# Loading x ahead of its tables, in pieces of 112 and 14 rows, and reordering the first weights: FNet mixing with a sigmoid GLU on one core

## The chip, the cores and the metric

The kernel runs on one core of a Trainium2 chip. The core has five engines that run side by side, each in the order of its own instruction list: TensorE (PE, matmuls; weight loads are listed as PEld), VectorE (DVE), ScalarE (ACT), GpSimd (POOL) and SyncE (SP), which here issues nearly all DMA transfers. They wait for each other through semaphores. The metric is device microseconds of one execution. The time before is 1924.73 us, the median of three runs (1924.28 to 1924.87).

## The reference

The input x has 8 sequences of 3008 positions with 256 features. It goes through a Fourier transform along the positions and one along the features, of which the real part is kept; then every position goes through a feed-forward layer with 1536 hidden units.

```python
X = np.fft.fft(x, axis=1)            # x: (8, 3008, 256)
X = np.fft.fft(X, axis=2)
x = X.real.reshape(8 * 3008, 256)
gate = 1.0 / (1.0 + np.exp(-(x @ w_gate)))     # w_gate, w_val: (256, 1536)
val = x @ w_val
out = (gate * val) @ w_out                     # w_out: (1536, 256)
```

## The kernel before

The order of every engine's work is written out by hand: the program order of the Python code is the order on each engine. Between engines, semaphores hold an instruction until what it reads has been written. Transfers on SyncE's queue are issued in program order too, and a transfer that has to wait holds back all behind it.

**Sequence transform.** Sine and cosine tables (`stab`, 126 rows on partitions, 6 slots `q`, two tables `t`) are multiplied with folded x. Symmetry is used: x is folded (`fold_ops`, L440) by adding and subtracting mirrored positions and features, so that each table has 126 x 6 rows. For the first sequence this goes in three thirds, two slots `q` each (`N3` = 3). For each third j VectorE does `third` (L498, L499, L460) and `feats` (L505 to L508); ScalarE makes signed copies, `turned` (L510) and a one-column form of it (L516). TensorE then adds the third's share to the sums: `e0_sums` (the `pe` matmuls, first eight straight ones for each third, then eight that read the turned copies), and three groups of `half` (the `ev` and `od` matmuls). The straight sums of a third read table `t` 0 or 1; the turned sums of odd `q` read the other one. A fourth group follows once all thirds are there. VectorE then adds `ev` and `od` into `pk` and `qk` (`places`, L584, L588).

**Weights.** `weight_load(j)` (L257) loads a block of 256 x 256 values of w_gate, w_val (j 0 to 11) or w_out (12 to 17), 0.5 MB each, from the eight-byte numbers in which the weights are given. `weight_parts(j)` makes two passes on ScalarE (L309, L311), `weight_join(j)` three on VectorE (L322, L323, L325) and one addition on GpSimd (L327) to turn them into four-byte numbers. `merge` (called `piece` at the start) multiplies the block with the feature-transform table `dt`, four matmuls into `ps`, and `merged(j)` copies the result to G on ScalarE (L358). `ge_load(j)` (L371) sends parts of a row of G to a column form `ge`.

**The steady loop.** For each of the steps i, TensorE makes `pf` from `pk` (`front_a`) and from `qk` (`front_b`); `seed` (L729) and `part` (L740) run on ScalarE, `gate_a` holds a sigmoid (L754) and VectorE's z (L755), `gate_b` VectorE's L767, a second sigmoid (L768) and VectorE's L771; `back` does the output matmuls. What is done besides (a weight's parts, join and use) is put into lists by step number: `pre` and `use` run after the gates of the step, `mid` (the join) inside `gate_b` or, at step 1, behind it. The list of pairs at L1053 gives each weight's step.

**The start, in SyncE's order** (L948 to L956): weights 0 to 3; then for each third its part of x (`load_third`, 1 MB, 128 partitions) and its two tables (`load_table`, 126 partitions, two slots of 377 values: 371 KB each); then weights 4 and 5. Eight `ge` transfers come next and wait for G, then weights 6 to 12. `dt` (256 KB) is issued by ScalarE (L947). TensorE starts with matmuls on a constant tile (`warm`). ScalarE does parts 0, 1, 2, then the copy to G of weight 0, then parts 3, and the copies 1 and 2. The parts of weight 4 come between the signed copies of the second and the last third.

Of the kernel before, what the change touches and what calls it, by code (L numbers as in the profile page):

```python
# [54 lines left out]
NP = 126  # L55
# [27 lines left out]
def kernel(  # L83
# [10 lines left out]
    nc = tc.nc  # L94
    B, _, _, _, D = xf.shape
    F = moe_w_gate.shape[1]
    P = 128
# [3 lines left out]
    NE = (M // 2) // 2 + 1  # L101
# [9 lines left out]
    N3 = NQ // 2  # L111
# [33 lines left out]
    def load_x(b):  # L145
        X[b] = xp.tile([P, 4, NQ, D], F32, name="x4", tag="x4")
        if b:
            for h in range(0, 4, 2):
                nc.sync.dma_start(out=X[b][:, h : h + 2], in_=XR[b][:, h : h + 2])

    def load_third(j):

        q = slice(2 * j, 2 * j + 2)
        rows = xf.rearrange("b p h q d -> (b p) h q d")
        nc.sync.dma_start(out=X[0][:, :, q], in_=rows[0:P, :, q])
# [26 lines left out]
    dt = const.tile([P, 2, D], F32, name="dt")  # L182
    HE, HO = M // 8 + 1, M // 8
# [4 lines left out]
    ST = [st[:, 0:n].rearrange("p (t q k) -> p t q k", t=2, q=NQ)]  # L188
# [13 lines left out]
    wkeep = dram.tile([P, 4, D], F32, name="wkeep")  # L202

    def load_table(t, j):
        q = slice(2 * j, 2 * j + 2)
        nc.sync.dma_start(out=ST[0][0:NP, t, q, 0 : HE + HO], in_=stab[:, t, q, HO : NE + HO])

    def table_again():

# [47 lines left out]
    def weight_load(j):  # L257


        w, c = jobs[j]  # L260
        src = (moe_w_gate, moe_w_val, moe_w_out)[w]
        src = src[2 * c * P : 2 * (c + 1) * P, :] if w == 2 else src[:, c * WC : (c + 1) * WC]
        src = src.rearrange("(c p) f -> p c f", p=P)

        def some(n, pool, tag):

            if tag not in shared:
                shared[tag] = pool.tile([P, n * WC], F32, name=f"w{tag}", tag=tag)
            return shared[tag]

        def home(j):

            if j in (0, 1, 2, 10, 11):
                t = hp.tile([P, 6 * WC], F32, name="raw", tag="h")
                return t[:, 0 : 4 * WC], t[:, 4 * WC :]
            if j in (3, 4):
                ws = some(5, pqp, "qk")[:, (j - 3) * 2 * WC : (j - 2) * 2 * WC]
                return sp.tile([P, 4 * WC], F32, name="raw", tag="sf"), ws
            if j < 8:
                t = wf[:, j - 4].rearrange("p m n -> p (m n)")  # L280
                return t[:, 0 : 4 * WC], t[:, 4 * WC : 6 * WC]
            if j < 10:
                shared[j] = cp.tile([P, 10 * WC], F32, name="wc", tag="c")
                return shared[j][:, 0 : 4 * WC], shared[j][:, 4 * WC : 6 * WC]
            return (shared[8][:, 6 * WC :] if j == 12 else shared["qk"][:, 0 : 4 * WC],
                    shared[9][:, (6 + 2 * (j - 12)) * WC : (8 + 2 * (j - 12)) * WC])

        if j < KEEP:
            raw, ws = home(j)
        else:  # L290
            both = some(24, xp, "x4").rearrange("p (i n) -> p i n", n=2 * WC)
            i = 3 * (j - KEEP)
            raw, ws = both[:, i : i + 2].rearrange("p a n -> p (a n)"), both[:, i + 2]
        raw = raw.bitcast(I32).rearrange("p (c f w) -> p c f w", c=2, w=2)
        ws = ws.rearrange("p (c f) -> p c f", c=2)
        WS[j] = ws
        if src.dtype == F32:
            nc.sync.dma_start(out=ws, in_=src)
        else:
            RAW[j] = raw  # L300
            nc.sync.dma_start(out=raw.rearrange("p c f w -> p c (f w)"), in_=src.bitcast(I32))

    def weight_parts(j, which=(0, 1)):

        if j in RAW:
            raw, ws = RAW[j], WS[j]
            lo, hi = raw[:, :, :, 0], raw[:, :, :, 1]
            if 0 in which:
                nc.scalar.activation(ws, hi.bitcast(F32), AF.Abs)  # L309
            if 1 in which:  # L310
                nc.scalar.activation(lo, lo.bitcast(U32), AF.Copy, scale=2.0 ** -29)  # L311

    def weight_join(j, other=None):
        if j not in RAW:
            return
        raw, ws = RAW.pop(j), WS[j]
        lo, hi = raw[:, :, :, 0], raw[:, :, :, 1]
        wi = ws.bitcast(I32)
        mid_ = bank("join", other).rearrange("p (c f) -> p c f", c=2)
        mi = mid_.bitcast(I32)  # L320
        ts = nc.vector.tensor_scalar
        ts(out=mid_, in0=ws, scalar1=2.0 ** -15, scalar2=HUGE, op0=ALU.max, op1=ALU.min)  # L322
        ts(out=mi, in0=mi, scalar1=3, scalar2=0x3FFFFFF8, op0=ALU.logical_shift_left,  # L323
           op1=ALU.bitwise_and)
        nc.vector.scalar_tensor_tensor(out=wi, in0=hi, scalar=-(2 ** 30), in1=mi,  # L325
                                       op0=ALU.bitwise_and, op1=ALU.bitwise_or)
        nc.gpsimd.tensor_tensor(wi, wi, lo, op=ALU.add)  # L327
# [25 lines left out]
    def merged(j):  # L353

        g, c = jobs[j]
        ps = MERGED.pop((g, c))
        cs = slice(c * WC, (c + 1) * WC)
        nc.scalar.copy(G[:, :, g, cs], ps.rearrange("p (h n) -> p h n", h=2))  # L358
# [12 lines left out]
    def ge_load(j):  # L371
        for g, f in ge_at((j,)):
            nc.sync.dma_start(out=ge[:, g, f : f + 1], in_=G2[0:1, g, f * P : (f + 1) * P])
# [233 lines left out]
    def e0_sums(j):  # L607

        if not j:
            E0["ps"] = bank("pe", NB - 1)  # L610
        for q in (2 * j, 2 * j + 1):
            for blk in range(2):
                row = (2 * blk + q % 2) * TB
                mm(E0["ps"][row : row + 1, columns(blk)[0]], W[0, blk][2][:, q], table_of(0, q, blk), not j, j == N3 - 1)
        for q in (2 * j, 2 * j + 1):
            for blk in range(2):
                row = (2 * blk + q % 2) * TB
                mm(E0["ps"][row : row + 1, columns(blk)[1]], XV[:, blk, q, HD : HD + 1],
                   table_of(0, q, blk, True), False, j == N3 - 1)
# [324 lines left out]
    nc.gpsimd.memset(nil, 0.0)  # L944
    nc.scalar.activation(table, nil[:, 0, 0:1], AF.Sigmoid)
    nc.gpsimd.dma_start(out=zero, in_=nil)
    nc.scalar.dma_start(out=dt, in_=dtab.rearrange("(c p) d -> p c d", p=P))  # L947
    load_x(0)  # L948
    for j in range(4):
        weight_load(j)  # L950
    for j in range(N3):
        load_third(j)
        for t in range(2):
            load_table(t, j)
    for j in (4, 5):
        weight_load(j)  # L956

    def warm(n):
# [5 lines left out]
    def piece(j, other=None):  # L964
        merge(WS.pop(j), *jobs[j], other)
# [4 lines left out]
    for j in range(4):  # L970
        weight_parts(j)
        weight_join(j, j % 3)
        piece(j, (None, None, None, 3)[j])
        if j > 1:
            merged(j - 2)
    merged(2)
    for j in range(3):
        ge_load(j)
    seq_start(0)
# [3 lines left out]
    for j in range(N3):  # L983
        folds[2 * j]()
        e0_sums(j)
        if not j:
            merged(3)
            ge_load(3)
            for i in (6, 7, 8, 9, 10, 11, 12):
                weight_load(i)  # L990
        folds[2 * j + 1]()
        if j == 1:
            weight_parts(4)
        for sums, _, _ in halves:
            sums(2 * j, 2 * j + 1)
# [53 lines left out]
    def using(j):  # L1049
        weight_use(j, j % 2)  # L1050
        if jobs[j][0] < 2:
            merged(j)
    for j, i in ((11, 1), (12, 3), (13, 5), (14, 6), (15, 8), (16, 10), (17, 12)):  # L1053
        if j > 10:
            pre.setdefault(i - 1, []).append(lambda j=j: weight_parts(j))
        mid.setdefault(i, []).append(lambda j=j: weight_join(j, 2))
        if jobs[j][0] == 2:
            use.setdefault(i + 2, []).append(lambda j=j: using(j))
# [138 lines left out]
```

## Time and profile before

| | |
|---|---|
| median of 3 runs | 1924.73 us (1924.28 to 1924.87) |
| the profiled execution's own time | 1925.47 us |
| its span, from the first to the last instruction | 1923.70 us |
| TensorE busy | 1912.1 us, 99% of the span |
| weight loads / VectorE / ScalarE / GpSimd busy | 93% / 73% / 70% / 81% |
| TensorE's first matmul on a weight | 9.33 us |
| TensorE's first `pe` sums | 19.04 us |
| turned `pe` sums of the last third | 31.12 us |
| last wait of TensorE in the start-up | ends at 60.20 us |

The page gives, for one execution, each engine's busy time, the chain of work that ended last, groups of instructions and the transfers. The same trace can be asked for a stretch of time: an instruction's line then holds its start and duration in us, engine, line of the code, operation, what is written and read, the shape, the count, and in square brackets how long the engine had been idle before it and who ended that. A line of the waits holds who waited for whom: us in total, times, the longest. A line of the stages holds a stretch, its length, the busy time of PE, PEld, DVE, ACT and POOL with the number of instructions, the granted TensorE clock, the mean busy share of the 16 DMA engines, and GB/s.

### The profile page before, as it was taken

Reading aid. Unit: us, or ns where it says so; the run is one execution under the profiler, and the core shown is the slowest. Engines: PE = TensorE matmul, PEld = TensorE weight load, DVE = VectorE, ACT = ScalarE, POOL = GpSimd, SP = SyncE. Lnnn points to the kernel's source line nnn. Section 1 sums busy time; section 2 is a strip of 40 time slices with the busy share of each in tenths; the row PEclk is TensorE's granted clock in tenths of the full one; section 3 lists DMA queues with packets and bytes.
Section 4 is the critical chain, followed back from the end, with each engine's and each line's share of the span. In section 5 each row is a group of like instructions: output and inputs, shape, how many; then the busy total and the mean of one; then the engine's idle time right before and its main releaser. Section 6 shows DMA issues by size and latency. Waiting matters only on the chain.

```text
span 1923.7 us, 34664 instructions
## 1 busy us (share of the span) xinstructions
PE 1912.1 (99%) x11340; PEld 1793.4 (93%) x11340; DVE 1410.9 (73%) x3220; ACT 1346.3 (70%) x3158; POOL 1554.7 (81%) x2807
## 2 busy tenths in 40 slices
PE   8999999999999999999999999999999999999999
PEld 7899999999999999999999999999999999999998
DVE  7757876787767776777777777777777777766776
ACT  5877767767777677776777767777677766777775
POOL 2589989978898688986888878988788886777775
PEclk9999999999999999999999999999999999999999
DMA  9251421111020201202111020111200100000001
GB/s 305 84 91 37 106 80 57 51 62 33 20 77 26 80 18 36 68 15 80 25 48 49 20 81 21 47 51 24 80 14 15 26 16 15 15 22 20 26 17 30
DMA packets 169215, 95.62 MB, mean 50 GB/s; under 512 B 129658, under 2 KB 159940, under 8 KB 167244
## 3 DMA queue, kind: packets, MB, share of 16 engines
q1 hardware_dynamic: 168482, 92.90, 17.0%
q8 instruction: 91, 1.49, 0.3%
q14 instruction: 88, 0.72, 0.1%
q10 hardware_dynamic: 522, 0.50, 0.1%
q0 software_dynamic: 32, 0.00, 0.0%
HBM read 68.13 MB, written 47.24 MB: 60 GB/s over the span
## 4 chain that ended last, share of the span: by engine, by line
PE 96%; ACT 1%; POOL 0%; DVE 0%; issue 0%; ACTq 0%; POOLq 0%
PE pf L135 50%; PE po L135 41%; PE ev L135 2%; PE rows L135 1%; PE od L135 1%; PE row L135 0%; POOL sf L777 0%; ACT pf L729 0%; ACT G L358 0%; ACT ae L740 0%; PE pe L135 0%; ACT wf L311 0%; ACT wc L311 0%; PE ps L135 0%; POOL st L231 0%
## 5 line engine op out<-in xcount | busy, mean ns | idle before, releaser
L777 POOL TENSOR_TENSOR sf<-h 128x168 f32<-128x168 f32 (+1 forms) x935 | 516.7, 571 | 229.8 <-DVE h L771 229.2
L777 POOL TENSOR_TENSOR sf<-h,sf 128x168 f32<-128x168 f32 (+1 forms) x1122 | 614.0, 568 | 49.4 <-DVE h L771 47.9
L135 PE MATMUL pf<-qk,G 128*128 128x252 f32 (+1 forms) x2304 | 582.0, 375 | 1.3 <-ACT ae L740 1.3
L135 PE MATMUL pf<-pk,G 128*128 128x252 f32 (+1 forms) x2304 | 582.5, 376 | 0.0
L729 ACT ACTIVATE pf<-ek,ge 128x252 f32<-128x252 f32 (+1 forms) x1152 | 542.6, 471 | 19.3 <-DVE h L771 0.3
L771 DVE TENSOR_TENSOR h<-pf,z 128x252 f32<-128x252 f32 (+1 forms) x576 | 241.6, 419 | 415.2 <-ACT pf L768 413.6
L135 PE MATMUL po<-sf,wf 128*128 128x168 f32 (+1 forms) x2992 | 516.9, 306 | 0.3 <-POOL sf L777 0.2
L740 ACT ACTIVATE ae<-pf 128x504 f32<-128x504 f32 (+1 forms) x576 | 339.2, 589 | 249.2 <-PE pf L135 248.0
L135 PEld LDWEIGHTS pf<-pk,G 128*128 128x128 f32 x2304 | 437.0, 190 | 51.7 <-issue 2.0
L135 PEld LDWEIGHTS po<-sf,wf 128*128 128x128 f32 x2992 | 460.6, 190 | 9.2 <-POOL sf L777 1.0
L135 PE MATMUL po<-h,wf 128*128 128x168 f32 (+1 forms) x2618 | 463.3, 305 | 0.0
L135 PEld LDWEIGHTS pf<-qk,G 128*128 128x128 f32 x2304 | 410.8, 190 | 27.9 <-ACT ae L740 2.1
L755 DVE TENSOR_TENSOR z<-ae,pf 128x504 f32<-128x504 f32 (+1 forms) x576 | 386.0, 670 | 63.1 <-ACT h L754 58.3
L135 PEld LDWEIGHTS po<-h,wf 128*128 128x128 f32 x2618 | 416.6, 190 | 16.2
L895 DVE TENSOR_TENSOR c<-c 128x168 f32<-128x168 f32 (+1 forms) x929 | 423.5, 464 | 3.4
L754 ACT ACTIVATE h<-pf 128x252 f32<-128x252 f32 (+1 forms) x576 | 218.5, 379 | 208.5 <-PE pf L135 199.8
L767 DVE TENSOR_TENSOR h<-h,pf 128x252 f32<-128x252 f32 (+1 forms) x576 | 233.5, 405 | 0.0
L768 ACT ACTIVATE pf<-z 128x252 f32<-128x252 f32 (+1 forms) x576 | 211.4, 367 | 23.4 <-DVE h L767 20.1
L777 POOL TENSOR_TENSOR sf<-sf 128x168 f32<-128x168 f32 (+1 forms) x187 | 104.2, 557 | 14.7
L777 POOL TENSOR_TENSOR sf<-sf,h 128x168 f32<-128x168 f32 (+1 forms) x187 | 110.3, 590 | 0.0
L808 ACT COPY c<-po 128x504 f32<-128x504 f32 (+1 forms) x141 | 80.0, 568 | 0.0
L904 DVE STREAM_TRANSPOSE os<-c 128x256 f32<-128x256 f32 x184 | 79.9, 435 | 0.0
(168 smaller groups left out, 921.9 us busy)
## 6 DMA issues: line engine op xcount, KB each, us to landing
x<-xr SPq DMA_DIRECT2D x14, 1536.0 KB
out_dram<-os SPq DMA_DIRECT2D x368, 56.0 KB
xr<-in_xf_dram SPq DMA_DIRECT2D x14, 768.0 KB
xr<-in_xf_dram SPq DMA_DIRECT2D x35, 256.0 KB
ek<-ed SPq DMA_DIRECT2D x39, 126.0 KB
out_dram<-os SPq DMA_DIRECT2D x284, 7.0 KB
x<-in_xf_dram SPq DMA_DIRECT2D x3, 1024.0 KB
st<-in_stab_dram SPq DMA_DIRECT2D x4, 564.8 KB
```

The costliest lines, as they stand in the source:

```text
L135: nc.tensor.matmul(o, l, r, start=start, stop=stop, skip_group_check=True)
L729: nc.scalar.activation(PF[i][:, g], EK[i // NFT], AF.Copy, scale=ge[:, g, f : f + 1])
L740: nc.scalar.activation(AP[i], PF[i], AF.Copy, scale=2.0)
L754: nc.scalar.activation(H[p][:, fh, 0:n], PF[i][:, 0], AF.Sigmoid)
L755: nc.vector.tensor_tensor(z[:, :, ::-1], AP.pop(i), PF[i], op=ALU.subtract)
L767: nc.vector.tensor_tensor(h[:, fh, 0:n], h[:, fh, 0:n], pf[:, 1], op=ALU.mult)
L768: nc.scalar.activation(pf[:, 0], z[:, 0], AF.Sigmoid)
L771: nc.vector.tensor_tensor(h[:, fh, n:], pf[:, 0], z[:, 1], op=ALU.mult)
L777: nc.gpsimd.tensor_tensor(block(p, dst), block(p, a), block(p, b), op=(ALU.subtract, ALU.add)[op])
L808: (nc.vector.tensor_copy if t == 1 or t == 3 and not last else nc.scalar.copy)(C[0][:, 3 * t * R : 3 * (t + 1) * R], PO[t][:, 0 : 3 * R])
L895: engine.tensor_tensor(t[:, dst * R : (dst + 1) * R], *v, op=(ALU.subtract, ALU.add)[op])
L904: nc.vector.transpose(os_[0][:, s, 0:nb, h, :], t[:, c0 : c0 + nb * TB])
```

## The change

All three thirds of x are issued ahead of all tables. The table transfers are cut to rows 0 to 111, and the remaining rows 112 to 125 of a table, for all six slots, go in one transfer of their own (14 rows of 6 x 377 values) ahead of that table's first piece. Weight 4 is issued between the tables of the second and the last third, and weights 6 and 7 move up behind 5, ahead of the eight `ge` transfers. `dt` moves from ScalarE's queue to SyncE's, behind the second weight. On ScalarE the first three copies to G come after the parts of weight 3, and weight 11 moves one step later: its parts from step 0 to step 1, its join from step 1 to inside the gate of step 2. TensorE's and GpSimd's orders stay as they were; on VectorE only weight 11's join moves, behind the next z (L755) and L767.

```diff
     def load_table(t, j):
-        q = slice(2 * j, 2 * j + 2)
-        nc.sync.dma_start(out=ST[0][0:NP, t, q, 0 : HE + HO], in_=stab[:, t, q, HO : NE + HO])
+        q, rows = slice(2 * j, 2 * j + 2), slice(0, NP - NP % 16)
+        if not j:
+            last = slice(NP - NP % 16, NP)
+            nc.sync.dma_start(out=ST[0][last, t, :, 0 : HE + HO], in_=stab[last, t, :, HO : NE + HO])
+        nc.sync.dma_start(out=ST[0][rows, t, q, 0 : HE + HO], in_=stab[rows, t, q, HO : NE + HO])
...
-    nc.scalar.dma_start(out=dt, in_=dtab.rearrange("(c p) d -> p c d", p=P))
     load_x(0)
     for j in range(4):
         weight_load(j)
+        if j == 1:
+            nc.sync.dma_start(out=dt, in_=dtab.rearrange("(c p) d -> p c d", p=P))
     for j in range(N3):
         load_third(j)
+    for j in range(N3):
+        if j == N3 - 1:
+            weight_load(4)
         for t in range(2):
             load_table(t, j)
-    for j in (4, 5):
+    for j in (5, 6, 7):
         weight_load(j)
...
         piece(j, (None, None, None, 3)[j])
-        if j > 1:
-            merged(j - 2)
-    merged(2)
+    for j in range(3):
+        merged(j)
...
-            for i in (6, 7, 8, 9, 10, 11, 12):
+            for i in (8, 9, 10, 11, 12):
                 weight_load(i)
...
-    for j, i in ((11, 1), (12, 3), (13, 5), (14, 6), (15, 8), (16, 10), (17, 12)):
+    for j, i in ((11, 2), (12, 3), (13, 5), (14, 6), (15, 8), (16, 10), (17, 12)):
```

## The prediction

> **What bounds the kernel now.** I read the page's busy shares and its chain first, then TensorE's waits up to 70 us and from there on, then the timeline, engine by engine, of the first 60 us, then the DMA rate by stage.
>
> ```profile
> PE 1912.1 (99%) x11340; PEld 1793.4 (93%) x11340; DVE 1410.9 (73%) x3220; ACT 1346.3 (70%) x3158; POOL 1554.7 (81%) x2807
> PE 96%; ACT 1%; POOL 0%; DVE 0%; issue 0%; ACTq 0%; POOLq 0%
> ```
>
> TensorE works for 1912.1 us of 1923.7 and holds 96% of the chain. Its matmuls stay as many, and in the same order. So the change can only alter TensorE's idle time, 11.6 us in all. The next fence is TensorE's waits before 70 us (the first four lines) and after 70 us (the last one): us in total, times, longest.
>
> ```profile
> PE ps L135 <- POOL wqk L327: 1.7, 1, 1.7
> PE pe L135 <- ACT st L516: 1.4, 1, 1.4
> PE pf L135 <- ACT ae L740: 1.3, 1, 1.3
> PE ps L135 <- POOL raw L327: 0.9, 1, 0.9
> ...
> PE po L135 <- POOL sf L777: 0.2, 1, 0.2
> ```
>
> Everything that can be won stands in the first 61 us, and it is some 5 us, 0.28% of the time. The three waits that the change reaches are of 1.7, 1.4 and 1.3 us. From 60.20 on the chain is TensorE alone, so the forecast is a shift of that point. Now the two waits in the middle, from the timeline:
>
> ```profile
> 25.11 0.17 DVE L498 TENSOR_TENSOR x<-x 126x4 f32<-126x4 f32 x1 [1.23 <-DMA x<-in_xf_dram]
> 29.68 0.66 ACT L309 ACTIVATE wqk<-raw 128x512 f32<-128x512 f32 x1 [3.06 <-DMA raw<-in_moe_w_gate_dram]
> 30.78 0.29 ACT L516 ACTIVATE st<-x,sgn 126x4 f32<-126x4 f32 x1
> 31.12 0.50 PE L135 MATMUL pe<-st 126*1 126x188 f32 x8 [1.36 <-ACT st L516]
> ```
>
> VectorE waits for x's last third until 25.11. ScalarE then waits for weight 4 until 29.68, and `turned`'s first copy for the last third (L516), in order behind it, keeps TensorE until 31.12. The third wait:
>
> ```profile
> 50.83 0.68 ACT L309 ACTIVATE raw<-raw 128x512 f32<-128x512 f32 x1
> 51.97 0.37 ACT L754 ACTIVATE h<-pf 128x252 f32<-128x252 f32 x1
> 54.32 0.68 DVE L322 TENSOR_SCALAR join<-raw 128x512 f32<-128x512 f32 x1
> 56.38 0.67 DVE L755 TENSOR_TENSOR z<-ae,pf 128x504 f32<-128x504 f32 x1
> 57.41 0.38 ACT L768 ACTIVATE pf<-z 128x252 f32<-128x252 f32 x1 [1.80 <-DVE h L767]
> 60.20 1.12 PE L135 MATMUL pf<-qk,G 128*128 128x252 f32 x4 [1.32 <-ACT ae L740]
> ```
>
> Weight 11's halves (L309) stand ahead of gate 0 on ScalarE, and its join (54.32 to 56.38) ahead of gate 1 on VectorE. The DMA rate by stage (the last two columns are share and GB/s):
>
> ```profile
> 9.50:12.00 2.50, 2.45 (x11) 1.84 (x12) 2.39 (x4) 0.64 (x2) 1.28 (x1) 1.00 1.06 400
> 12.00:15.50 3.50, 3.36 (x15) 2.30 (x13) 2.88 (x7) 1.71 (x4) 1.96 (x2) 1.00 1.09 241
> 18.50:22.00 3.50, 3.48 (x31) 2.36 (x30) 3.40 (x6) 2.28 (x5) 0.00 (x0) 1.00 1.06 279
> ```
>
> x moves at 400 GB/s, the tables (12 to 15.5, 18.5 to 22) at 241 to 279, though the queues are full in all three stretches.
>
> **The change part by part.** Times are those of the profiled execution: 1925.47 us with 1.77 us around its span of 1923.70, 0.74 above the median of 1924.73. The shift is added to the median.
>
> *Tables behind x.* TensorE's sums of the first third need its tables as well as x. Before, both were there when TensorE came free, at 19.04. Now three thirds of x go first. By the DMA rates summed over half microseconds the first four weights and `dt` (2.36 MB) are through at 8.7. Three thirds (3.15 MB) at 400 GB/s take 7.9 us more: 16.6. Before, x's last third stopped moving at about 24.1 (the rate falls to 233 GB/s there) and was seen at 25.1, so I add 1.0 for the slowest part: x is in SBUF at 17.6. Then two pairs, 14 rows (127 KB) and 112 rows (338 KB), must land before the turned sums can start, since odd q use the other table.
>
> A 112-row transfer: at 400 GB/s 0.85 us; it can't cost more than a whole 126-row one. Of those, two and a weight fill 25.11 to 29.68. With 1.3 us for the weight (0.52 MB at 400) a table took 1.65. I take 1.3, its bytes at the 260 GB/s between the two table stretches. A 14-row transfer: 0.3 at 400 GB/s, or 1.65, a whole table's, if its few rows are no faster. No row is near it; I take 1.1, in the upper half, because these tables already ran well below the full rate.
>
> The second pair lands at 17.6 + 2 x (1.1 + 1.3) = 22.4; ends 17.6 + 2 x (0.3 + 0.85) = 19.9 and 17.6 + 4 x 1.65 = 24.2. Before, the turned sums started at 19.36. So TensorE starts them 3.0 us later, and idles from about 18 on.
>
> The Trainium skill speaks against the 14-row pieces: SBUF — State Buffer, "Door 1: the DMA port swizzle", puts partitions 112 to 125 on 4 of 16 write ports, at about 27 GB/s each. By that a piece would take an estimated 1.3 us (four rows of 9 KB on one port) and the pair would land at 22.8, the shift below 0.4 larger. The trace of before writes no such narrow range, so no run here shows it.
>
> *What the thirds then gain.* Before, the turned sums go from 19.36 (first third) to 31.12 (last), 11.8 us. With the tables of later thirds 1.3 us apart behind the first, x's folds done by about 27 (three folds of 4.2 to 5.1 us from 13.6) and weight 4 landed at about 26.4, ahead of ScalarE's need at 28.3, no wait is left but TensorE itself. 24.15 to 29.26 is one third, 5.1; 19.36 to 24.15 the first, 4.8; 0.3 for the straight sums; less 0.3 of small waits for VectorE: 9.9. The last third's turned sums then start at 22.4 + 9.9 = 32.3, against 31.12: **+1.2 us**. The 1.23 us of VectorE, the 3.06 us of ScalarE and TensorE's 1.36 are gone, paid for by the wait for tables. What follows to 50.04 hangs on these sums (VectorE's copies L644, at 31.74 before, then joins and places) and shifts whole.
>
> *Weight 11 one step later.* ScalarE: gate 0's sigmoid (L754) no longer waits for two halves (50.83 to 51.97) but for TensorE's `pf` (50.04 + 1.12): about 0.8 earlier. VectorE's z for it is held by weight 10's join (to 51.86): 0.5 earlier. Weight 11's halves (1.14) now come before gate 1's sigmoid, 55.0 for 54.35; but z of gate 1 no longer waits for the join: 55.4 for 56.38, L768 56.4 for 57.41, and L740, which TensorE awaits, 58.5 for 59.56. That is **-1.0 us**; bounds: 0, if the gate chain is held elsewhere, and -1.3, the whole wait. Behind the moved join waits gate 1's last product (L771), 58.5 for 57.83, read only by sums that run later. Weight 11's add on POOL ends near 60.0; TensorE asks near 60.8.
>
> *Parts that cost or bring nothing.* `dt` leaves ScalarE's queue (0.49 us of issue while ScalarE was idle till 4.99) for SyncE's: the first weights come up to 0.65 us sooner (0.26 MB at 400). Weight 3's halves no longer sit behind the first copy to G: they ran at 11.84, and could at about 9.5. Both let the join of weight 3 and the fold start about 1.1 us sooner and TensorE's fourth piece start at 16 instead of 17.11. Their cover is the wait for tables; with tables at 19.9 they would count. SyncE issues three more transfers, `dt` among them (0.4 to 0.5 us each where its queue has room), some 5 us ahead of need. Weights 6 and 7 pass eight `ge` loads that held the queue from 19.60 to 31.45; they are used at 36.60 and 39.56, so hidden. `ge` and weights 8 to 12 queue behind them, issued near 33 as before (32.65), used from 41.43. POOL's order is unchanged.
>
> Sum: +1.2 - 1.0 = +0.2, so 1924.73 + 0.2 = **1924.9 us**.
>
> **The rivals.**
> *The tables come quickly*: both kinds at the full rate, pair at 19.9. The shift is 2.5 less: 1922.4. For it: fewer rows in one transfer; against it: 241 GB/s with full queues.
> *The move of weight 11 brings nothing* because another wait (weight 10's join) holds gate 0: +1.2, 1925.9. For it: z was already held 0.5; against it: L768's 1.80 us is exactly the join.
> *The change does not do what it says*: a piece of 112 rows, and one of 14, is no quicker than a whole table of 126 rows. Pair at 24.2, 1.8 later: 1926.7. For it: the rate of 241 GB/s; against it: fewer bytes.
> *TensorE loses its clock*, the case that ends slower. Place: between the fourth piece's end at 18 and 22.4 it has 0.4 us of work. In the first stage 2 to 4 us held 6 matmul records and 6 to 8 us held 11, so a slow start of some 4 us works at about half speed. One more such stretch costs 4 x (1 - 6/11) = 1.8: 1926.7. It decides, over 0.2% (3.85 us) with the +0.2, when the slow time passes 8 us of the 14 that the sums take. Against it: the idle 1.7 us at 15.4 left the granted clock at 1.00.
> The Trainium skill (TensorE: Matmul & The Clock Gate, Part 1) halves the clock after an idle window of about 3.4 us; the two gaps here are an estimated 2 us each, so by it the clock holds unless the second pair is late.
>
> **How the numbers follow.** A measurement of this kernel can tell about 0.2%, 3.85 us, from no change. Chances: a wash near +0.2 0.56; quick tables 0.17; weight 11 for nothing 0.10; pieces no quicker 0.07; the clock 0.10. Every case but a long loss of clock lies within 3.85 us. Faster needs more than the idle it can reach (the 1.7, 1.4 and 1.3 add to 4.4, and the new wait must be nought): 0.02. Slower: 0.04, the long slow clock or a pair landing past 26. Same: 0.94. The range goes from the quick tables, 1922.4, to the +1.8 of the clock or of late tables on top of the sum, 1926.7, with 0.3 added for runs that differ by 0.6 (1924.28 to 1924.87): 1922.1 to 1927.0.
>
> **What would show it.** After: TensorE's list of waits names a DMA of `st` for `pe`, 2 to 4 us in total; VectorE's 1.23 for x and ScalarE's 3.06 for weight 4 are gone; the last third's turned sums start near 32.3; TensorE's wait for L740 is under 0.5. Wrong: turned sums of the first third before 21 (tables quicker) or after 24, matmuls of 0.64 us where 0.32 stood (the clock), a new wait behind weight 11.

## The result, and the profile after

The changed kernel takes **1928.56 us** (median of 20 runs, 1927.12 to 1929.58) against 1924.70 us for the kernel before (20 runs beside it). The ratio is 1.0018, 95% interval [1.0012, 1.0024]: slower by 3.86 us, just inside the 0.2% that was called no change, and 1.6 us above the predicted range. The profiled execution took 1927.58 us with a span of 1925.8, so it lies 1.0 below the median; the one of before lay 0.74 above its own. That is why the two profiles stand only 2.1 us apart.

The page of the changed kernel: busy time, then the chain of work that ended last, by engine.

```profile
PE 1914.1 (99%) x11340; PEld 1795.0 (93%) x11340; DVE 1410.0 (73%) x3220; ACT 1346.5 (70%) x3158; POOL 1554.3 (81%) x2807
PE 97%; DMA 1%; SPq 1%; POOL 0%; ACT 0%; DVE 0%; issue 0%; ACTq 0%; DVEq 0%; POOLq 0%
```

The matmuls are as many as before, but TensorE is busy 2.0 us longer (1912.1 before): some of them ran slower. TensorE's waits in the first 70 us of the changed kernel (us in total, times, longest):

```profile
PE pe L135 <- DVE x L463: 2.7, 1, 2.7
PE ps L135 <- POOL wqk L330: 1.0, 1, 1.0
PE pe L135 <- DMA st<-in_stab_dram: 1.0, 1, 1.0
PE ps L135 <- POOL raw L330: 0.4, 1, 0.4
```

The first line is the wait for the first pair of tables as well: VectorE had ended the L463 that it names at 17.47, 3.5 us earlier. (Lines after L206 are shifted by 3: L743 is L740 of before, L312 is L309.) The waits behind ScalarE (L516) and for L740 are gone. Now the `pe` and first `ev`/`od` sums from TensorE's timeline, and ScalarE's passes over weight 4:

```profile
20.93 0.50 PE L135 MATMUL pe<-st,x 126*1 126x189 f32 x8 [2.69 <-DVE x L463]
22.69 0.79 PE L135 MATMUL pe<-st 126*1 126x188 f32 x4 [0.95 <-DMA st<-in_stab_dram]
23.41 1.00 PE L135 MATMUL ev<-st,x 126*128 126x189 f32 x2
...
26.41 0.48 PE L135 MATMUL od<-st,x 126*128 126x188 f32 x2
...
28.74 0.50 PE L135 MATMUL pe<-st,x 126*1 126x189 f32 x8
...
34.16 0.50 PE L135 MATMUL pe<-st 126*1 126x188 f32 x8
...
62.20 1.12 PE L135 MATMUL pf<-qk,G 128*128 128x252 f32 x4
```

```profile
31.11 0.66 ACT L312 ACTIVATE wqk<-raw 128x512 f32<-128x512 f32 x1
```

The second pair of tables lets TensorE go on at 22.69, close to the 22.4 forecast. But the last third's turned sums start at 34.16, not at 32.3. Two `ev` matmuls take 1.00 us at 23.41 where the same two took 0.59 before. From the last third's sums to the end everything shifts whole: span minus start is 1925.8 - 34.16 = 1891.6 here and 1923.7 - 31.12 = 1892.6 before, and the 1.0 between them is weight 11's wait. ScalarE no longer idles ahead of weight 4 (3.06 us before).

The granted clock of the changed kernel, in stretches that begin and end where its records change or would change, each 3.41 us long (columns: stretch, length, busy PE, PEld, DVE, ACT, POOL with instructions, granted clock, DMA share, GB/s):

```profile
15.84:19.25 3.41, 1.99 (x8) 1.44 (x8) 3.30 (x7) 0.90 (x3) 0.35 (x1) 1.00 1.11 247
19.25:22.67 3.42, 0.81 (x12) 0.33 (x13) 3.27 (x6) 0.00 (x0) 0.00 (x0) 1.00 1.08 231
22.67:26.08 3.41, 3.39 (x12) 2.78 (x13) 3.30 (x7) 1.52 (x3) 0.00 (x0) 0.50 1.08 299
```

In the kernel before:

```profile
15.29:18.70 3.41, 1.73 (x8) 1.43 (x8) 3.29 (x5) 0.89 (x2) 1.77 (x1) 1.00 1.02 352
```

After a stretch with 0.81 us of matmuls TensorE worked at half its clock for 3.41 us, though no single gap was longer than 2.7 us. Before, the emptiest stretch held 1.73 us, and the clock stayed.

The mean clock over a whole run is listed for every run. One half-speed stretch takes 3.41 x 0.5 / 1926 = 0.0009 off it; the last 2 us or so of a run, at half clock when the matmuls end, take up to 0.0006 more. Of the 20 runs of the changed kernel 6 show 0.999, like the profiled one with its one slow stretch (mean 1927.75 us), and 14 show 0.998 (mean 1928.71): by that sum most of these lose two stretches.

### The profile page after: what moved, and what is told of

The parts are those of the page before. It is cut to its first block, busy times and chain, and to the rows that moved or that the text cites. A ratio compares the mean times of both kernels' runs of the same rounds, so it can differ in the third digit from the quotient of the medians.

```text
span 1925.8 us, 34670 instructions
## 1 busy us (share of the span) xinstructions
PE 1914.1 (99%) x11340; PEld 1795.0 (93%) x11340; DVE 1410.0 (73%) x3220; ACT 1346.5 (70%) x3158; POOL 1554.3 (81%) x2807
## 4 chain that ended last, share of the span: by engine, by line
PE 97%; DMA 1%; SPq 1%; POOL 0%; ACT 0%; DVE 0%; issue 0%; ACTq 0%; DVEq 0%; POOLq 0%
PE pf L135 50%; PE po L135 41%; PE ev L135 3%; PE rows L135 1%; PE od L135 1%; DMA st<-in_stab_dram 1%; PE row L135 0%; DMA wx<-in_moe_w_out_dram 0%; POOL sf L780 0%; PE pe L135 0%; PE ps L135 0%; SPq L304 0%; SPq L208 0%; SPq L155 0%; SPq L209 0%
## 5 line engine op out<-in xcount | busy, mean ns | idle before, releaser
L743 ACT ACTIVATE ae<-pf 128x504 f32<-128x504 f32 (+1 forms) x576 | 339.2, 589 | 249.0 <-PE pf L135 247.8
```

The costliest lines, as they stand in the source:

```text
L743: nc.scalar.activation(AP[i], PF[i], AF.Copy, scale=2.0)
```

## The experiments

My first theory: the loss is TensorE's clock, which falls in the wait for tables. The rival: the tables land later than estimated (the pieces, or something else in the loading order). The kernel before was run beside each group; its medians were 1924.6 to 1924.9. The interval of each ratio is some 0.0009, or 1.7 us, either way; so a step of about 1 us below rests on its trace, or on several pairs that agree, and not on one median.

**The clock held by filler matmuls.** Six matmuls on a constant tile, read by nobody, go into the wait.

```diff
+    fill = bank("fill")
     for j in range(N3):
         folds[2 * j]()
+        if not j:
+            for _ in range(6):
+                mm(fill[:, 0:CH], busy[:, 0:P], busy, True, True)
         e0_sums(j)
```

> The changed kernel with six more matmuls on the constant tile (about 2.5 us, into a bank of their own, read by nobody) on TensorE between the fourth piece and the first sums, where it idled from 18.2 to 20.9. Theory (the clock): the changed kernel lost its time because TensorE ran at half clock from 22.67 to 26.08, right when its tables had come. With the filler the granted clock stays at 1.00, the matmuls of the first third are back at 0.32 us, the second third's sums start near 27.5 instead of 28.74, and the time falls by 1.3 us (one half-clock stretch, as in the profile) to 3 us (two): 1925.6 to 1927.3. Rival (the tables alone): the clock record is an echo of the wait, nothing is won, 1928.5.

Measured: 1926.76 us, 1.8 less than the changed kernel; ratio to before 1.0010 [1.0002, 1.0019]. Its timeline (the trace counts each of the six matmuls as two):

```profile
18.15 2.71 PE L135 MATMUL fill<-busy 128*128 128x252 f32 x12
23.41 0.49 PE L135 MATMUL pe<-st 126*1 126x188 f32 x4 [1.33 <-DMA st<-in_stab_dram]
28.14 0.50 PE L135 MATMUL pe<-st,x 126*1 126x189 f32 x8
33.57 0.50 PE L135 MATMUL pe<-st 126*1 126x188 f32 x8
```

The tables were later in this execution than in the changed kernel's (23.41 for 22.69), and still the first third took 28.14 - 23.41 = 4.7 us for 28.74 - 22.69 = 6.05, and the last third's sums came 0.6 earlier. So adding work made the kernel faster: the clock costs 1.8 us of the median, 1.0 against the changed kernel's runs at 0.999 and 1.95 against those at 0.998. It doesn't explain the other 1.9 by which the changed kernel is above before, or some 3 with weight 11's gain put back.

**Weight 11 alone, and taken back.** In the kernel before (e2_w11_only), and reversed in the changed one (e3_no_w11):

```diff
-    for j, i in ((11, 1), (12, 3), (13, 5), (14, 6), (15, 8), (16, 10), (17, 12)):
+    for j, i in ((11, 2), (12, 3), (13, 5), (14, 6), (15, 8), (16, 10), (17, 12)):
```

> The kernel before with weight 11's move alone. Theory (worth 1.0 us by itself): TensorE's wait of 1.3 us at 60.20 goes, time 1923.7 where the kernel before has 1924.7. Rival (only worth something when other parts of the change are there): 1924.7.

> The changed kernel with weight 11 back at step 1 (its parts at step 0, its join at step 1). Theory (its move won 1.0 us, as forecast): TensorE's wait of 1.3 us for L743 ahead of the third step's pf comes back, time 1.0 us over the changed kernel, about 1929.5. Rival (the join was held elsewhere anyway): as the changed kernel, 1928.5.

Alone it gives 1923.69 us (0.9993 [0.9984, 1.0001]); without it the changed kernel takes 1929.45 (1.0025 [1.0015, 1.0036]), and the old wait is back in its list:

```profile
PE pf L135 <- ACT ae L743: 1.3, 1, 1.3
```

The move is worth 1.0 to 1.2 us by the one and 0.9 by the other. The forecast was 1.0.

**The pieces.** The changed kernel with whole tables of 126 rows (e4_whole), and the kernel before with the pieces but its old order (e7_split):

```diff
-        q, rows = slice(2 * j, 2 * j + 2), slice(0, NP - NP % 16)
-        if not j:
-            last = slice(NP - NP % 16, NP)
-            nc.sync.dma_start(out=ST[0][last, t, :, 0 : HE + HO], in_=stab[last, t, :, HO : NE + HO])
-        nc.sync.dma_start(out=ST[0][rows, t, q, 0 : HE + HO], in_=stab[rows, t, q, HO : NE + HO])
+        q = slice(2 * j, 2 * j + 2)
+        nc.sync.dma_start(out=ST[0][0:NP, t, q, 0 : HE + HO], in_=stab[:, t, q, HO : NE + HO])
```

> The changed kernel with each table again as one transfer of 126 rows, x still ahead of all tables. Theory (the narrow 14-row pieces, 0.9 to 1.05 us each in the changed kernel, cost more than the 112-row pieces save): the first pair lands after 2 x 1.65 instead of 4.5 us, about 1.2 us earlier, turned sums near 21.5; the time falls by 1.2 us, and by 1 to 2 us more if the shorter gap keeps the clock: 1925.5 to 1927.4. Rival (the whole tables are as slow, because they leave engines unused): 1928.5 or more.

> The kernel before with the tables split as in the changed one (14 rows of both thirds' tables first, then 112 rows), in the old order between the thirds of x, nothing else. From the changed kernel's trace a 14-row piece costs about 1.0 and a 112-row piece about 1.2; a whole one cost about 1.65. My theory: the first pair lands some 1.2 us later, still ahead of TensorE (free at 19.04); x's last third comes 0.4 later and weight 4, behind all six pieces, 0.7 earlier (2 x 1.0 - 6 x 0.45); so ScalarE's wait for weight 4 shrinks by 0.7 and the time is 1924.2, -0.7. Rival (the pieces cost together what e4_whole showed, 1.35 more for the first pair and no gain after it): weight 4 comes up to 1.3 later and the last third's turned sums at 32.4: 1926.2.

e4_whole: 1925.87 us (1.0003 [0.9994, 1.0012]), 2.7 less than the changed kernel. Its turned sums of the first third start at 21.25 for 22.69:

```profile
21.25 0.79 PE L135 MATMUL pe<-st 126*1 126x188 f32 x4 [0.94 <-DMA st<-in_stab_dram]
```

e7_split: 1926.22 us (1.0011 [1.0002, 1.0020]), 1.6 above before and not 0.7 below it: the rival was right. The pieces delay the first pair in the old order too; there TensorE's first sums start at 20.36 (19.04 before), and the stretch of 14.21 to 17.63 us held only 1.22 us of matmuls, with the same consequence:

```profile
14.21:17.63 3.42, 1.22 (x6) 0.77 (x5) 3.37 (x6) 0.59 (x1) 2.23 (x1) 1.00 1.04 296
17.63:21.04 3.41, 3.41 (x19) 2.01 (x21) 3.28 (x7) 0.87 (x2) 0.00 (x0) 0.50 1.09 303
```

So cutting the tables in two costs in both orders; no run showed it to win.

**Whole tables and fillers together.** e4_whole with the fillers of e1_fill:

> The changed kernel with whole tables (e4_whole, 1925.87) and the six filler matmuls of e1_fill between the first fold and the first sums. My theory: the clock no longer falls, and half to one and a half of a window's 1.7 us is won: 1924.4 to 1925.2, granted clock 1.00 in 20 to 30 us. What is left over e2_w11_only (1923.69) is the idle time for tables behind x, 0.7 to 1.5. Rival (in e4_whole the slow window cost nothing since the sums waited for data anyway, so all 0.9 between e1_fill and e4_whole is the pieces' size): 1925.8 as e4_whole.

1925.12 us, as expected from the first theory; in its profile the granted clock is 1.00 throughout. With the clock held, the pieces still cost 1926.76 - 1925.12 = 1.6 us.

**Two better orders that were none.** Whole tables between the thirds of x, weight 4's halves behind the last third's first copy (e5_order); and the same with pieces, the two small ones issued at the very start from ScalarE's queue (e6_tails):

```diff
-    for j in range(N3):
-        load_third(j)
-    for j in range(N3):
-        if j == N3 - 1:
-            weight_load(4)
-        for t in range(2):
-            load_table(t, j)
+    load_third(0)
+    for t in range(2):
+        load_table(t, 0)
+    load_third(1)
+    load_third(2)
+    for t in range(2):
+        load_table(t, 1)
+    weight_load(4)
+    for t in range(2):
+        load_table(t, 2)
...
+        if j == 2:
+            weight_parts(4)
         folds[2 * j + 1]()
-        if j == 1:
-            weight_parts(4)
```

> This kernel is the changed one with whole tables of 126 rows, put between the thirds of x (x 0, pair 0, x 1, x 2, pair 1, weight 4, pair 2), and weight 4's halves moved on ScalarE behind the last third's fold; the moves of dt, of the copies to G and of weight 11 stay. My theory (the wait for tables and the clock that falls in it are the whole loss; the rest of the change is worth -1.0 to -1.2): the first pair is there at 15.6, ahead of TensorE, so no wait for a table, granted clock 1.00 throughout, the last third's turned sums at about 30.0 (31.12 before) as ScalarE's wait for weight 4 is no longer ahead of them, weight 11's wait gone: -1.1 - 1.2, so 1922.6, 0.999 of before. Rival 1 (the earlier sums win nothing because TensorE then waits for weight 4's join, later): 1923.7, as the weight 11 move alone. Rival 2 (the moves of dt and of the copies cost something): 1924.5 or more.

> The order of e5_order, but each table in rows of 112 as in the changed kernel, with the two 14-row pieces issued at the very start from ScalarE's queue, beside the first weights. Theory A (the pieces are cheap when they run beside other transfers): pairs land about 0.8 earlier each than whole ones, x and weight 4 up to 2 us earlier, no wait for tables, last third's turned sums at 29.0, 1921.3 to 1922.3. Theory B (14-row pieces hold up whatever runs beside them, as they held 0.9 to 1.0 us each in the changed kernel): the first weights and so the fold start about 2 us later, but that is covered until the last third's sums; time as e5_order, 1922.6, or up to 1 us above.

1924.37 and 1925.09 us, where 1922.6 was expected. In e5_order I had put two thirds of x ahead of the second pair, and TensorE waited for that pair in place of the first. Its stretch with the least work (the last line below) held 1.72 us, and the clock stayed:

```profile
24.34 0.50 PE L135 MATMUL pe<-st,x 126*1 126x189 f32 x8 [0.96 <-DMA st<-in_stab_dram]
25.87 0.49 PE L135 MATMUL pe<-st 126*1 126x188 f32 x4 [0.73 <-DMA st<-in_stab_dram]
```

```profile
22.92:26.33 3.41, 1.72 (x20) 0.61 (x19) 3.30 (x7) 0.00 (x0) 0.00 (x0) 1.00 1.07 263
```

In e6_tails the small pieces held up the first weights: ScalarE began at 6.30 us, in e5_order at 4.83, and the first sums at 20.88 for 18.20. But e5_order, 0.7 above e2_w11_only, also met its second rival: the moves of `dt` and of the copies to G might cost something. The prediction had put both at nothing.

**`dt` and the copies to G alone, in the kernel before.**

```diff
-    nc.scalar.dma_start(out=dt, in_=dtab.rearrange("(c p) d -> p c d", p=P))
     load_x(0)
     for j in range(4):
         weight_load(j)
+        if j == 1:
+            nc.sync.dma_start(out=dt, in_=dtab.rearrange("(c p) d -> p c d", p=P))
...
-        if j > 1:
-            merged(j - 2)
-    merged(2)
+    for j in range(3):
+        merged(j)
```

> The kernel before with only dt on SyncE's queue and the first copies to G behind the fourth weight's halves. My prediction put these at nothing, but named the wait for tables as their cover, and in this order no wait for tables is there. Theory A (the last third's turned sums wait for weight 4 by way of ScalarE, which these moves don't touch): the fourth piece starts about 1 us earlier on TensorE (near 16), the first sums about 1 us earlier, the last third's turned sums where they stood: 1924.7, within 0.3 of before. Theory B (the second third's sums come earlier and something of it goes through): 1923.7. Theory C (dt on SyncE's queue makes x's thirds and weight 4 later): up to 1925.5.

All three theories failed: 1927.95 us, 1.0017 [1.0008, 1.0026], as slow as nearly the whole change. Its VectorE, ScalarE and TensorE:

```profile
26.19 0.17 DVE L498 TENSOR_TENSOR x<-x 126x4 f32<-126x4 f32 x1 [2.37 <-DMA x<-in_xf_dram]
30.52 0.66 ACT L309 ACTIVATE wqk<-raw 128x512 f32<-128x512 f32 x1 [4.79 <-DMA raw<-in_moe_w_gate_dram]
31.96 0.50 PE L135 MATMUL pe<-st 126*1 126x188 f32 x8 [2.48 <-ACT st L516]
```

```profile
29.03:32.45 3.42, 0.94 (x15) 0.22 (x15) 1.32 (x3) 1.39 (x3) 0.00 (x0) 1.00 0.37 85
32.45:35.86 3.41, 3.41 (x13) 3.41 (x12) 3.13 (x8) 2.72 (x6) 0.00 (x0) 0.50 0.57 162
```

The first sums did come 0.9 earlier (18.16 us), but x's last third came 1.1 later (26.19 for 25.11) and weight 4 0.8 later (30.52 for 29.68). TensorE's wait behind ScalarE grew from 1.36 to 2.48, and in it the clock fell. Which of the two moves does it was taken apart next: `dt` alone (e14_dt_only), and `dt` put back in the changed kernel (e12_dt_back, the two `dt` lines above reversed).

> The kernel before with dt as SyncE's third transfer instead of the first of ScalarE's queue; nothing else. Theory dt (one queue less makes the tables' transfers slower): x's last third 1 us later, weight 4 1 us later, TensorE's wait behind ScalarE 2.4 for 1.4, 1927.0 to 1928.0, as e9_act_order (1927.95). Theory copies (the copies to G behind the fourth weight's halves do it): 1924.7.

> The changed kernel with dt back on ScalarE's queue, nothing else. Theory dt: the second pair lands 1 us earlier, near 21.8 to 22.3; the clock still falls in the wait for it: 1927.0 to 1927.7 for 1928.56. Rival (with x first dt's queue doesn't matter, or dt being later than weight 1 there even helped the first pieces): 1928.3 to 1929.

`dt` alone: 1927.15 us, 1.0013 [1.0004, 1.0022], 2.5 above before; its runs spread from 1925.0 to 1930.0, and its profile, at 1925.16, is one of the quickest, so where a usual run loses its time was not seen. e9_act_order, with the copies to G as well, lies 0.8 above it, which is within the noise. The changed kernel with `dt` back: 1927.40, 1.2 less. Of its 11 runs 7 show the clock 0.999 (mean 1927.06) and 4 show 0.998 (1928.32): 0.7 and 0.4 below the changed kernel's at the same clock; and 0.998 is rarer (14 of 20 there), though 11 runs are few to prove that. In its profile the second pair lets TensorE go on only 0.2 earlier and the last third's turned sums start 0.4 earlier than in the changed kernel's:

```profile
22.49 0.79 PE L135 MATMUL pe<-st 126*1 126x188 f32 x4 [1.11 <-DMA st<-in_stab_dram]
33.79 0.50 PE L135 MATMUL pe<-st 126*1 126x188 f32 x8
```

And with whole tables and fillers (e8_whole_fill, `dt` back):

> The changed kernel without its other costs: whole tables, the six filler matmuls that hold the clock, dt on ScalarE's queue. What is left of the change is x ahead of the tables, the copies to G, weight 11. Against e8_whole_fill (1925.12) theory dt expects 0.7 to 1.3 less: 1923.8 to 1924.4, so x first costs nearly nothing against e2_w11_only (1923.69). Rival (dt's queue doesn't matter in this order): 1925.1.

1924.45 us, 0.7 less than e8_whole_fill, and all 11 runs within 0.23 us: the tables are there before TensorE asks, which fits runs so alike.

```profile
17.96 2.71 PE L135 MATMUL fill<-busy 128*128 128x252 f32 x12
20.92 0.50 PE L135 MATMUL pe<-st 126*1 126x188 f32 x8
```

The turned sums follow the straight ones here without a wait for a table; in e8_whole_fill half of them waited for one:

```profile
21.65 0.49 PE L135 MATMUL pe<-st 126*1 126x188 f32 x4 [0.27 <-DMA st<-in_stab_dram]
```

The fillers hold TensorE until about 20.6 in both; whether fewer of them would do, and start the sums sooner, was not tried.

**The quickest version.** Weight 11 one step later and weight 4's halves behind the last third's copies (e10_parts4), then with the copies to G as well (e13_best), or with `dt` too (e11_both); loads in the old order, whole tables:

```diff
-        if j == 1:
+        if j == 2:
             weight_parts(4)
...
-        if j > 1:
-            merged(j - 2)
-    merged(2)
+    for j in range(3):
+        merged(j)
...
-    for j, i in ((11, 1), (12, 3), (13, 5), (14, 6), (15, 8), (16, 10), (17, 12)):
+    for j, i in ((11, 2), (12, 3), (13, 5), (14, 6), (15, 8), (16, 10), (17, 12)):
```

> The kernel before with weight 11 one step later (1923.69 alone) and weight 4's halves behind the last third's copies on ScalarE instead of ahead of its first one; loads in the old order. If ScalarE's wait for weight 4 was the whole of TensorE's 1.0 to 1.4 us ahead of the last third's turned sums, these start 0.3 after the straight ones, 1.0 to 1.2 earlier, with no wait: 1922.5 to 1922.7. Rival (another operand is as late, or weight 4's join later holds the heads): 1923.5 to 1924.5.

> e9_act_order and e10_parts4 together: weight 11, weight 4's halves, dt and the copies to G moved, x and the tables loaded as before. If the first sums come 1 us earlier and nothing of DMA stands behind them (x's last third is folded at about 26.5 and TensorE asks for it at about 28.9), another 0.7 to 1.1 is won: 1921.5 to 1921.9, granted clock 1.00. Rival (x's last third and its fold hold the sums): as e10_parts4, 1922.6. Rival (dt on SyncE's queue delays the first table pair or x): 1923 or more.

> e10_parts4 (1923.37: weight 11 and weight 4's halves moved) with the copies to G behind the fourth weight's halves, dt left on ScalarE's queue. Theory dt: loads are as quick as in e10_parts4, the first sums come 1 us earlier, x's last third is folded in time: 1922.3 to 1922.8. Theory copies (they make the loads later): 1924.4, as e11_both.

Measured: 1923.37, 1924.36 and **1922.92** us (0.9996, 0.9999 and 0.9993, this one [0.9984, 1.0002]). The first two fell 0.7 and more short of what was hoped for. e13_best lies 1.7 us under before and 5.6 under the changed kernel; but its interval against before just reaches 1, so a gain over before is likely and not shown. Its sums run through without a wait, 2.6 us earlier than in the profile of before:

```profile
18.29 0.50 PE L135 MATMUL pe<-st 126*1 126x188 f32 x8
28.51 0.50 PE L135 MATMUL pe<-st 126*1 126x188 f32 x8
```

The time gains less than that, since at least 0.8 goes to two short waits further on (0.5 for L740, 0.3 for a weight's join) and the profile of before was 0.7 late. e11_both differs from e13_best by `dt`'s queue alone and is 1.4 us slower. In its profile VectorE gets x's last third at 25.78 us instead of 23.83, and half of the last turned sums wait for a table until 29.82. VectorE's waits for x, in e11_both and then in e13_best (us in total, times, longest):

```profile
DVE x L498 <- DMA x<-in_xf_dram: 2.7, 2, 2.0
DVE x L498 <- DMA x<-in_xf_dram: 1.0, 1, 1.0
```

With e14_dt_only (2.5), e12_dt_back (1.2) and e15_whole_fill_dt (0.7) this is the fourth pair of kernels in which this one move costs time.

## Why the prediction was wrong

The medians, step by step (the third line takes several parts together, and a step depends on the order in which they are taken):

| step | kernel | median, us | step, us |
|---|---|---|---|
| the kernel before | | 1924.70 | |
| weight 11 later | e2_w11_only | 1923.69 | -1.0 |
| + x ahead of whole tables, copies to G, weight 4 and the weights behind it earlier, fillers | e15_whole_fill_dt | 1924.45 | +0.8 |
| + `dt` on SyncE's queue | e8_whole_fill | 1925.12 | +0.7 |
| + tables in pieces | e1_fill | 1926.76 | +1.6 |
| + no fillers: the clock | the changed kernel | 1928.56 | +1.8 |

*Right: where the bound lies.* The time is a shift of the last third's turned sums and of weight 11's wait: span minus that start is 1891.5 to 1891.6 in e1_fill, e2_w11_only and the changed kernel, and 1892.6 in the kernel before, which still has that wait.

*Right: weight 11, -1.0.* Measured 0.9 to 1.2.

*Right in sum, by luck: the pieces.* Forecast were 4.8 us for the first two pairs of pieces, and their packets in the trace run from 16.1 to 21.0. But both terms were off: the 14-row pieces took 0.87 and 0.64 us where 1.1 stood, the 112-row ones 1.9 each where 1.3 stood, and the errors cancel. For this pair the rival "no quicker than a whole table" held for the larger pieces: two whole tables span 3.7 us in e8_whole_fill, two 112-row pieces 1.88 + 1.91 = 3.8, and the small ones come on top. A whole table was taken as 1.65, so the estimate itself implied 1.5 for the cut, and e1_fill against e8_whole_fill gives 1.6. Two smaller errors cancel as well: the tables' first packets moved beside x's last ones, and TensorE went on 1.7 us after the last packet, where 1.0 had been allowed. The Trainium skill's rule on ports (SBUF — State Buffer, "Door 1: the DMA port swizzle") had given an estimated 1.3 us for a 14-row piece: the packets of the two took 0.87 and 0.64 us, so less than the estimate. The 112-row pieces of the first pair took 133 to 139 ns a packet; the same shape later took 96 to 98. Why the first pair is slower stays open.

*The step that failed first: "the clock holds".* The rival had the right place and the right price, 1.8 us, and was given 0.10. The price is partly luck: one slow stretch cost 1.25 in the profile (the first third took 6.05 us for a forecast of 4.8), and most of the runs behind the median lose two by their mean clock. The rival was argued away by two things. The idle time was read gap by gap ("two gaps ... an estimated 2 us each"), and the 1.7 us at 15.4 that had left the clock at 1.00 was taken as evidence. The traces show that the work in a fixed stretch of 3.41 us counts, not a gap: see the last section. That earlier stretch had held 1.73 us of work, just above the border. The range, too, allowed the clock's 1.8 or late tables, not the clock with anything else. The rule of the Trainium skill that was cited beside it (TensorE: Matmul & The Clock Gate, Part 1: half clock after an idle window of about 3.4 us) has the length of the window right. Read as "no gap of 3.4 us", it would keep the clock here; the trace has the clock halved after gaps of 2.7 and 0.95 with 0.81 us of work around them, so the measurement decides against that reading.

*The step that failed second: "parts that cost or bring nothing".* `dt` was costed as 0.65 us sooner for the first weights, hidden by the wait for tables. The sign was wrong. In the changed kernel the move costs 1.2 us by the medians, in e8_whole_fill 0.7, alone 2.5. Where its path was seen, the loads behind it land later (x's last third 1.95 us later in e11_both than in e13_best); in the changed kernel's two profiles only 0.2 to 0.4 of the 1.2 shows. The copies to G were not taken back in the changed kernel; in the old order, with weight 4 out of the way, they go with 0.4 less (e13_best against e10_parts4), a step that is within the noise.

*The step that failed third: the profile against the median.* The shift was added to the median, but the profile of before was late by 0.74 in the very point it was measured from. In e2_w11_only, profiled at its median, the last third's sums start at 30.44, not at 31.12, with the same path. So some 0.7 of the shift was missing from the start. On the other side the changed kernel's profile lies 1.0 under its median, mostly since it lost one stretch of the clock and most runs, by the mean clock, two.

*Small:* the 9.9 us for the thirds counted on 0.3 of small waits that didn't go: e1_fill, at full clock, took 33.57 - 23.41 = 10.2.

Together: the sums were to come 1.2 later and came 3.86 + 1.0 = 4.9 later by the medians, 3.7 more. In the profiles the last third's turned sums start at 34.16 for 32.3, 1.9 late: 0.3 from the second pair (22.69 for 22.4), 1.25 from the clock, 0.3 from the small waits. To that come the 1.0 by which this profile lies under its median and the 0.74 by which the other lay above its own: 3.6. `dt` is no term of its own in this sum. Counted by medians, its 1.2 and the clock's 1.8 overlap with the rest, since a shorter wait loses the clock less often.

## What to carry to other kernels

Where a change makes TensorE wait, count its work in every stretch of 3.4 us and not the longest gap; when less than half of one could be filled, price the wait with another 1 us for a lost stretch and 2 us for two, as here, or fill it with idle matmuls. A transfer moved to another queue has a price of its own even when its bytes are the same and it lands ahead of need: look at what queues behind it, and run the move alone. Before times are read off one profile, see where that execution stands in its runs, and which part of it was late.

## What the runs showed of the hardware

**The clock goes by work in a fixed grid of 3.413 us.** In all 17 profiles the clock first becomes full between 4.0 and 7.4 us, and every later change lies a whole number of 3.413 us behind that. Cut by that grid, the first 35 us of each profile give one border. Matmul time (busy PE) in a stretch and the clock granted in the next:

| kernel | stretch, us | busy PE, us | next clock |
|---|---|---|---|
| changed | 19.25 to 22.67 | 0.81 | 0.50 |
| e12_dt_back | 18.70 to 22.11 | 0.81 | 0.50 |
| e9_act_order | 29.03 to 32.45 | 0.94 | 0.50 |
| e3_no_w11 | 19.64 to 23.05 | 1.10 | 0.50 |
| e7_split | 14.21 to 17.63 | 1.22 | 0.50 |
| e4_whole | 17.59 to 21.00 | 1.52 | 0.50 |
| e5_order | 22.92 to 26.33 | 1.72 | 1.00 |
| before | 15.29 to 18.70 | 1.73 | 1.00 |
| e10_parts4 | 14.61 to 18.02 | 1.79 | 1.00 |

Every other stretch after the first held 1.87 or more, and none was followed by a slow one. The border lies between 1.52 and 1.72 of 3.41, near half. The longest gap doesn't decide: e4_whole lost the clock with none above 1.19 us, and the kernel before kept it after one of 1.68. Where the grid lies changes from run to run, so the same wait can be slow in one run and not in another: of e4_whole's 11 runs 9 show 0.999 (mean 1925.89 us) and 2 show 1.000 (1924.24). The kernel before may be touched by it too: of the 33 runs beside the last group 10 show a clock of 0.999, with a mean of 1925.23 us for 1924.50 at 1.000; but the last microseconds alone can give 0.999, and no slow stretch of it was profiled.

**The queue of one early transfer changes the speed of later ones.** With `dt` on ScalarE's queue the 1508-byte packets of the tables took 84 to 89 ns on average in the old order (before, e2_w11_only, e10_parts4, e13_best), with `dt` on SyncE's 93 to 95 (e9_act_order, e11_both, e14_dt_only); 1512 packets on 16 engines make 0.4 to 1.0 us of that, about what x's last third and weight 4 come later. With x first and whole tables, the first pair's packets span 3.1 us in e15_whole_fill_dt and 3.7 in e8_whole_fill. In the changed kernel, with pieces, the packets are no quicker with `dt` back, though the time is. Why a 256 KB transfer whose packets have ended by 6.5 us does this to packets from 11 us on was not settled.
